# A fused attention and feed-forward kernel: fewer filler matmuls in slot 0, one turned product moved a slot later, one key copy moved behind a sum

## The chip, the cores and the metric

The kernel runs on one core of one Trainium2 chip. The metric is the device time of one execution in microseconds, the median of several runs. Besides the runs there is one profiled execution, whose trace is read here.

## The reference

Inputs are q, k, v of shape 8 x 8 x 576 x 64 (batch, heads, sequence, head width), a forget gate f of 8 x 8 x 576, and two weight matrices, 512 x 2048 and 2048 x 512. Cut to what matters:

```python
scores = scale * q @ k.T                          # per batch and head
cum = np.cumsum(np.log(np.clip(f, 1e-4, 1)), -1)
decay = cum[..., :, None] - cum[..., None, :]
attn = softmax(where(causal, -1e9, scores + decay))
x = (attn @ v) -> (8 * 576, 8 * 64)               # heads side by side
h = x @ w_in
out = (h - tanh(h)) @ w_out                       # 4608 x 512, float32
```

## The kernel before

**Slots.** A pair is two heads of one batch element; there are 32 pairs, four to a batch element (NPAIR = 4). The main loop at the end of the kernel goes over slots p = 0, 1, 2, ...; slot p emits the work of pair p. `att_items(p)` writes that work as a list of items by hand, going over the seven score tiles of a pair (ti = 0 to 6). Between the items the loop deals out pieces of the feed-forward part (the list `mlp`): how many a slot gets is in `TAKE`, and `first` says after how many counted items the dealing begins. Nothing is reordered afterwards: each engine runs its instructions in the order in which they are emitted, and waits on semaphores for its inputs and for buffers to come free. Slots 0 to 3 (batch element 0) have no feed-forward work yet, since it needs the finished attention of batch element 0; it begins in slot 4.

**One pair.** `trans` turns the queries or keys of a pair on TensorE (six transposing matmuls, L298) into a PSUM bank, and two copies, for the even and the odd positions, bring the bank into QT or KT (L309 on ScalarE, L311 on VectorE). The string `copies` names the engines: V is VectorE, A is ScalarE. With "VA" only the first copy is emitted at once and the second is put on the list `LATER`, which `rest` empties; with other strings both are emitted at once. `scores` multiplies (L352; in batch element 0 a second matmul, L355, adds the causal mask), and ScalarE takes the exponential into an e tile (L361; el is the small fourth tile). From batch element 1 on GpSimd masks e instead (L371). `values` multiplies e with v (L389) and then has VectorE divide by the row sums in three steps: L398 (rs), L399 (reciprocal), L400 (xn, the product of the pair).

**Turning the products.** The feed-forward part needs xn with the features on the partitions. In batch element 0 `turn` does this with five transposing matmuls (L417) into a bank and one copy into the ring XR, on VectorE when it is called with `vector=True` (L419), else on ScalarE (L421). In later batch elements a transposing DMA does it. The four pairs of batch element 0 fill XR chunks 0 to 3. Before the change pair 0 is turned in slot 2, pair 1 in slot 3 (both by VectorE), pair 2 and pair 3 in slot 4 (by ScalarE and VectorE).

**Feed-forward.** `mlp1(u, ft)` projects 512 tokens (block u) onto 128 hidden features with four matmuls, one for each XR chunk (L451, hps); ScalarE takes tanh (L456, th), and VectorE forms the gated sum gq = hps + th, with th = tanh(-h) (L462). The first two units, (0, 0) and (0, 1), are split in slot 4: part 0 does the matmuls of chunks 0 to 2, and part 1, at ti = 4 and 5, the one of chunk 3, tanh and sum. `mlp2_plain` and `mlp2` (L492, L517) multiply with the second weights. The PSUM banks m0 to m2 go round among turned tiles and projections through `m_bank`; scores go round two banks "sc" and one bank "tr".

**Unread matmuls.** `unread(n)` issues n matmuls of 128 x 128 on a constant tile into the bank "tr" (L566, idle <- warm); nobody reads the result. They stand at the start (47, 6, 38, 2) and in slot 0 (6, 4, 10 after the tiles ti = 2, 5, 6).

**Loads.** All loads of q, k, v and the weights are DMAs that GpSimd's queue issues in program order between its masks; SyncE issues the small rows, the transposing DMAs and the output.

Of the kernel before, what the change touches and what calls it, by code (L numbers as in the profile page):

```python
# [21 lines left out]
def kernel(  # L22
# [18 lines left out]
    NPAIR = H // 2  # L41
# [28 lines left out]
    def m_bank(name):  # L70
        while M_AT[0] % 3 in KEPT:
            M_AT[0] += 1
        M_AT[0] += 1
        return ps_m.tile([P, 512], FP32, tag=f"m{(M_AT[0] - 1) % 3}", name=name)

    def keep():
        while M_AT[0] % 3 in KEPT:
            M_AT[0] += 1
        KEPT.append(M_AT[0] % 3)
# [13 lines left out]
    qn, kn = ([t[0:S // NT6, :].rearrange("p (h n d) -> p h n d", h=H, n=NT6) for t in raw] for raw in (qraw, kraw))  # L93
# [3 lines left out]
    KT = [qkp.tile([D + 3, H, PITCH], FP16, tag=f"KT{i}", name=f"KT{i}") for i in range(2)]  # L97
# [100 lines left out]
    def load_aug(b):  # L198
        for to, of in aug_rows(b):
            nc.sync.dma_start(out=to, in_=of)  # L200

    def const_rows(i):
        h0 = 1 - i
        nc.sync.dma_start(out=QT[i][D:D + 2, h0:H, :], in_=minus16[0:2 * (H - h0), :])
        nc.sync.dma_start(out=KT[i][D + 2:D + 3, h0:H, 0:S], in_=ones16[0:H - h0, :])
# [81 lines left out]
    def trans(b, c, src, dst, early, copies, split=False):  # L287
        pn, g3 = S // NT6, NT6 // 2
        if early:
            t32 = m_bank("t32")  # L290
        elif KEPT and src is kn:
            t32 = ps_m.tile([P, UW], FP32, tag=f"m{KEPT[0]}", name="t32")
        else:
            t32 = ps_tr.tile([P, UW], FP32, tag="tr", name="t32")
        t16 = t32.bitcast(FP16)[:, 0:2 * S // 2].rearrange("p (a g n) -> p a g n", a=2, g=g3)
        for a in range(2):
            for g in range(g3):
                nc.tensor.transpose(out=t16[:, a, g, :],  # L298
                                    in_=src[b % 2][:, 2 * c + a, 2 * g:2 * g + 2, :],
                                    identity=id16[0:pn, 0:pn])  # L300
        parts = [(a, e) for a in range(2) for e in range(2)] if split else [(slice(0, 2), e) for e in range(2)]

        def copy(a, e, eng):
            if split:
                a = slice(a, a + 1)
            to = dst[b % 2][0:D, 2 * c:2 * c + 2, e:S:2].rearrange("d a (p g) -> d a p g", g=g3)[:, a]
            of = t16[e * D:(e + 1) * D, :, :, :].rearrange("d a g p -> d a p g")[:, a]
            if eng == "A":
                nc.scalar.activation(out=to, in_=of, func=AF.Copy)  # L309
            else:  # L310
                nc.vector.tensor_copy(out=to, in_=of)  # L311

        todo = [lambda a=a, e=e, eng=eng: copy(a, e, eng) for (a, e), eng in zip(parts, copies)]
        now = 1 if copies == "VA" else 2
        for fn in todo[:now]:
            fn()
        if copies == "VA":
            LATER.extend(todo[now:])
        return todo[now:]

# [117 lines left out]
    def widen(n):  # L438
        turn_of[:] = [n, 0]
# [123 lines left out]
    def unread(n):  # L563
        idle = ps_tr.tile([P, UW], FP32, tag="tr", name="idle")
        for i in range(n):
            nc.tensor.matmul(out=idle[:, i % 4 * P:i % 4 * P + P], lhsT=warm, rhs=warm, start=True, stop=True)  # L566

    pairs = [(b, c) for b in range(B) for c in range(NPAIR)]

    def start():  # L570
        unread(47)
        nc.scalar.activation(out=QT[0][NH:NX, 0, :], in_=cum[NH:NX, :], func=AF.Identity, bias=add_q[NH:NX, :], scale=mul_q[NH:NX, :])
        q_rest = trans(*pairs[0], qn, QT, True, "AAAA", True)
        for fn in q_rest:
            fn()
        unread(6)
        k_rest = trans(*pairs[0], kn, KT, True, "VVVV", True)
        unread(38)
        scores(*pairs[0], 0)
        for fn in k_rest:  # L580
            fn()
        scores(*pairs[0], 1)
        unread(2)
# [7 lines left out]
    def att_items(p):  # L591
        def put(fn, *args):
            items.append((lambda: fn(*args), True))

        items = []
        here = pairs[p] if p < len(pairs) else None
        before = pairs[p - 1] if 0 < p <= len(pairs) else None
        after = pairs[p + 1] if p + 1 < len(pairs) else None
        early = p < NPAIR
        for ti in range(len(TILES)):  # L600
            if here and (p > 0 or ti > 1):
                put(scores, *here, ti)
            if p == 1 and ti == 6:
                items.append((lambda: const_rows(1), False))
                items.append((lambda: load_aug(1), False))
            if p == 0 and ti in (2, 5, 6):
                put(unread, {2: 6, 5: 4, 6: 10}[ti])
            if p == 1 and ti == 3:
                put(last)
            for load in LOADS.get((p, ti), ()):  # L610
                items.append((load, False))
            at_q, at_k = (1, 2) if p == 0 else (None, 0) if early else (0, 2) if p == NPAIR else (0, 3)
            if ti == 5 and p < NPAIR - 1:
                put(trans, *pairs[p + 2], qn, QT, True, "VV")
            if p in (2 * NPAIR - 1, 2 * NPAIR, 2 * NPAIR + 1) and (ti % 2 or ti == 0):
                items.append((rest, False))
            if p in (2 * NPAIR - 1, 2 * NPAIR) and ti % 2 == 0:
                pair = pairs[2 * NPAIR + 2 * (p - 2 * NPAIR + 1) + ti // 4]
                put(trans, *pair, *((kn, KT) if ti % 4 else (qn, QT)), False, "VA")
            if ti == at_q and p < 2 * NPAIR - 1:  # L620
                put(trans, *after, qn, QT, early, "VV")
            if p == NPAIR:
                if ti in (4, 5):
                    put(mlp1, 0, ti - 4, 1)
            if ti == at_k and p < 2 * NPAIR - 1 and p != NPAIR:
                put(trans, *after, kn, KT, early, "AV" if p in (0, 2) else "VV")
            if p == NPAIR:
                if ti == 1:
                    put(turn, *pairs[p - 2])
                    put(values, *before)  # L630
                    put(mlp1, 0, 0, 0)
                elif ti == 2:
                    put(mlp1, 0, 1, 0)
                    put(turn, *before, True)
                    put(trans, *after, kn, KT, early, "VV")
            elif early and ti in (2, 4) and before:
                put(values, *before, (ti // 2 - 1,))
            elif not early and ti == 2 and before:
                put(values, *before, (0, 1), p == NPAIR + 2)
            if p < NPAIR:  # L640
                if ti == 1 and p > 1:
                    put(turn, *pairs[p - 2], True)
            elif p > NPAIR and ti == 3:
                items.append((release, False))
                put(turn, *before)
        return items
# [4 lines left out]
    TAKE = (0, 0, 0, 0, 2, 7, 6, 6, 6, 8, 8, 7, 7)  # L651
    at = 0
    start()
    bulk()
    for p in range(len(pairs) + 1):
        b, c = divmod(p, NPAIR)
        items = att_items(p)
        take = TAKE[p] if p < len(TAKE) else 8 - (p - len(TAKE)) % 2
        if p == 2 * NPAIR - 1:
            keep()  # L660
        if p == 2 * NPAIR + 1:
            KEPT.clear()
            widen(1)
        mine = mlp[at:at + take]
        at += take
        first = 14 if p == NPAIR else 0
        if p == len(pairs):
            for fn, *args in mine[0:2]:
                fn(*args)
            mine = mine[2:]  # L670
        given, n = 0, 0
        whole = sum(counts for _, counts in items)
        for emit, counts in items:
            emit()
            n += counts
            while n > first and given < len(mine) and given * (whole - first) < (n - first) * len(mine):
                fn, *args = mine[given]
                fn(*args)
                given += 1
# [31 lines left out]
```

## Time and profile before

| | |
|---|---|
| time, median of 3 runs | 339.54 us (339.47 to 339.68) |
| profiled execution, its own time | 339.82 us |
| its span, first to last instruction | 338.1 us |
| TensorE (PE) busy | 331.3 us, 98% |
| VectorE (DVE) busy | 261.6 us, 77% |
| ScalarE (ACT) busy | 232.9 us, 69% |
| GpSimd (POOL) busy | 162.3 us, 48% |

Busy times are of the span of the profiled execution; what lies around the span (1.7 us) is not in the trace. Slot 0 begins near 9.5 us, pair 1's scores at 14.31, pair 2's at 17.65, pair 3's at 21.78, pair 4's at 25.71 and pair 5's at 34.22. In the lines of the trace PE is the matmuls, PEld TensorE's weight loads. "out<-in" names the tiles; x10 behind an operation means ten of them merged into one line. The line numbers are those of the kernel before.

### The profile page before, as it was taken

The page shows a single profiled execution, that of the slowest core. Times are in us where ns is not written, and L with a number is a line of the kernel's source. Part 1 is how long each engine was busy: PE and PEld are TensorE (multiplying, and loading weights), DVE is VectorE, ACT ScalarE, POOL GpSimd, SP SyncE. Part 2 cuts the span into 40 slices and gives each one's busy share as a digit, 9 for nine tenths or more (in the row PEclk, how much of TensorE's full clock was granted, in tenths as well). Part 3 has the DMA queues.
Part 4 walks back from the last instruction along what each step waited for, and adds up shares of the span by engine and source line. Part 5 has one row for each costly group of instructions (what it writes and reads, how often), then busy time and mean ns, then how long its engine had stood idle before and what let it go on. Part 6 is the DMA issues. An engine that isn't in the chain of part 4 may idle for free.

```text
span 338.1 us, 8750 instructions
## 1 busy us (share of the span) xinstructions
PE 331.3 (98%) x3325; PEld 237.7 (70%) x3325; DVE 261.6 (77%) x510; ACT 232.9 (69%) x437; POOL 162.3 (48%) x321
## 2 busy tenths in 40 slices
PE   8998999999999999999999999999999999999996
PEld 8875558875587558855888888656875686486485
DVE  7899886659888887778867796688667866966865
ACT  6896777978977886778677867787558733632630
POOL 8977467775667574777377637632322210000000
PEclk9999999999999999999999999999999999999999
DMA  9999999999969997999899999990130222002003
GB/s 112 143 202 201 186 198 170 172 156 168 141 88 169 153 134 81 133 181 135 100 110 186 129 115 110 168 132 16 50 114 3 19 66 95 2 31 95 1 12 114
DMA packets 147468, 38.82 MB, mean 115 GB/s; under 512 B 128181, under 2 KB 146335, under 8 KB 147426
## 3 DMA queue, kind: packets, MB, share of 16 engines
q0 software_dynamic: 94528, 18.37, 74.3%
q1 hardware_dynamic: 52892, 19.89, 32.5%
q8 instruction: 26, 0.43, 0.6%
q14 instruction: 16, 0.13, 0.2%
q10 hardware_dynamic: 6, 0.01, 0.0%
HBM read 36.85 MB, written 9.44 MB: 137 GB/s over the span
## 4 chain that ended last, share of the span: by engine, by line
PE 95%; DVE 2%; ACT 2%; issue 0%; ACTq 0%
PE hps L451 36%; PE ops L517 29%; PE ps L352 12%; PE av L389 8%; PE ops L492 4%; PE idle L566 3%; PE t L298 2%; ACT e L361 1%; DVE KT L311 1%; PE ps L355 0%; ACT KT L309 0%; PE x L417 0%; DVE XR L419 0%; DVE xn L400 0%; DVE QT L311 0%
## 5 line engine op out<-in xcount | busy, mean ns | idle before, releaser
L451 PE MATMUL hps<-XR,win 128*128 128x512 f16 (+1 forms) x640 | 140.7, 357 | 0.4 <-DVE gq L462 0.3
L456 ACT ACTIVATE th<-hps 128x512 f32<-128x512 f32 x144 | 86.7, 602 | 55.3 <-PE hps L451 52.3
L361 ACT ACTIVATE e<-ps 128x512 f16<-128x512 f32 x192 | 110.1, 597 | 9.8 <-PE ps L352 7.6
L462 DVE TENSOR_TENSOR gq<-hps,th 128x512 f16<-128x512 f32 x144 | 98.2, 687 | 23.5 <-ACT th L456 21.8
L371 POOL TENSOR_SCALAR_AFFINE_SELECT e<-e 128x128 f16<-128x128 f16 x168 | 59.9, 359 | 73.5 <-ACT e L361 71.4
L451 PEld LDWEIGHTS <-win 128*128 128x128 f16 x640 | 57.8, 97 | 48.9 <-issue 1.0
L352 PE MATMUL ps<-QT,KT 67*128 67x64 f16 (+4 forms) x384 | 76.5, 276 | 1.1 <-ACT e L361 0.8
L517 PEld LDWEIGHTS <-gq 128*128 128x128 f16 x640 | 60.3, 97 | 11.1
L517 PE MATMUL ops<-wout,gq 128*128 128x256 f16 x512 | 63.2, 272 | 0.0
L352 PEld LDWEIGHTS <-KT 67*128 67x128 f16 x384 | 36.5, 98 | 22.0 <-DVE KT L311 0.5
L389 PEld LDWEIGHTS <-e 128*128 128x128 f16 x896 | 32.3, 97 | 3.6
L389 PE MATMUL av<-vn,e 128*128 128x65 f16 x896 | 33.6, 193 | 0.0
L517 PE MATMUL ops<-W,sq 128*128 128x256 f16 x256 | 31.2, 272 | 0.0
L131 POOL DMA_DIRECT2D vn<-in_v_dram x32 | 28.0, 877 | 6.4 <-DMA win<-in_moe_w_in_dram 2.7
L400 DVE TENSOR_TENSOR xn<-av,rs 128x640 f16<-128x640 f32 x32 | 26.4, 825 | 1.3 <-DMA out_dram<-ost 0.2
L517 PEld LDWEIGHTS <-sq 128*128 128x128 f16 x256 | 24.2, 98 | 3.4
L108 POOL DMA_DIRECT2D kn<-in_k_dram x25 | 21.2, 846 | 2.1 <-issue 1.8
L108 POOL DMA_DIRECT2D qn<-in_q_dram x25 | 21.2, 846 | 1.8 <-issue 1.4
L371 POOL TENSOR_SCALAR_AFFINE_SELECT el<-el 128x128 f16<-128x128 f16 x28 | 9.3, 332 | 26.1 <-ACT el L361 25.9
L398 DVE TENSOR_SCALAR rs<-av 128x10 f32<-128x10 f32 x32 | 5.2, 163 | 18.4 <-PE av L389 17.3
L484 DVE TENSOR_TENSOR gq<-gq 128x512 f16<-128x512 f16 x32 | 17.1, 534 | 0.0
L532 ACT ACTIVATE m<-ops 128x512 f32<-128x512 f32 x16 | 9.5, 596 | 10.9 <-PE ops L517 10.9
(83 smaller groups left out, 316.2 us busy)
## 6 DMA issues: line engine op xcount, KB each, us to landing
out_dram<-ost SPq DMA_DIRECT2D x34, 256.0 KB
vn<-in_v_dram POOLq DMA_DIRECT2D x24, 128.0 KB, 6.0
qn<-in_q_dram POOLq DMA_DIRECT2D x20, 128.0 KB, 4.6
kn<-in_k_dram POOLq DMA_DIRECT2D x20, 128.0 KB, 5.3
win<-in_moe_w_in_dram POOLq DMA_DIRECT2D x2, 1024.0 KB, 11.6
wout<-in_moe_w_out_dram POOLq DMA_DIRECT2D x2, 1024.0 KB, 16.2
XR<-xn SPq DMA_TRANSPOSE x56
qn<-in_q_dram POOLq DMA_DIRECT2D x6, 144.0 KB, 4.8
```

The source lines that it names most:

```text
L108: nc.gpsimd.dma_start(out=dst[b % 2][0:pn, n, :].rearrange("p (h d) -> p h d", h=H), in_=src[b, :, n * P:n * P + pn, :].rearrange("h p d - ...
L131: nc.gpsimd.dma_start(out=vn[b % 2][:, n, h0:h1, 0:D], in_=v[b, h0:h1, n * P:(n + 1) * P, :].rearrange("h p d -> p h d"))
L352: nc.tensor.matmul(out=ps[:, col:col + n], lhsT=kt[0:rows, h, j * P:(j + 1) * P], rhs=qt[0:rows, h, i0:i0 + n], start=True, stop=cut == 0)
L361: nc.scalar.activation(out=e[:, lo:hi], in_=ps[:, lo:hi], func=AF.Exp, bias=-SHIFT, scale=qscale)
L371: nc.gpsimd.affine_select(out=view, in_=view, compare_op=ALU.is_ge, fill=0.0, base=0, pattern=pat, channel_multiplier=-1)
L389: nc.tensor.matmul(out=av[:, a, ib, :], lhsT=E.pop((b, c, a, j, ib)), rhs=vn[b % 2][:, j, 2 * c + a, 0:D + 1], start=(j == 0), stop=(j == ib))
L400: nc.vector.tensor_tensor(out=xn.rearrange("p i (a d) -> p a i d", a=2), in0=av[:, :, :, 0:D], in1=rs.to_broadcast([P, 2, NJ, D]), op=ALU. ...
L451: nc.tensor.matmul(out=hps[:, o:o + n], lhsT=win[:, ci, ft * P:(ft + 1) * P], rhs=XR[:, ci, t:t + n], start=(ci == 0), stop=(ci == NCH - 1))
L456: nc.scalar.activation(out=th, in_=hps, func=AF.Tanh, scale=-1.0)
L462: nc.vector.tensor_tensor(out=GQ[(u, i)][:, half, kt, :], in0=hps, in1=th, op=ALU.add)
L484: nc.vector.tensor_tensor(out=LHS[name](u, i)[:, ks], in0=LHS[x](u, i)[:, ks], in1=LHS[y](u, i)[:, ks], op=op)
L517: nc.tensor.matmul(out=ps[:, m, :], lhsT=LHS[lhs](u, kt // 4)[:, kt % 4, m * P:(m + 1) * P], rhs=rhs[:, kt, :], start=(fresh and (apart or ...
```

## The change

There are three edits.

1. `unread(38)` ahead of the first scores becomes `unread(34)`, and the 10 unread matmuls after the last score tile of slot 0 become 2: twelve fewer.
2. Pair 1's product is turned in slot 4, at ti = 0 behind the scores and the turned queries of that place, instead of in slot 3 at ti = 1; its copy into XR is done by ScalarE instead of VectorE. As slot 4 thereby has one more counted item, `first` goes from 14 to 15.
3. The copies of pair 5's turned keys, in slot 4 at ti = 2, are marked "Vv": the first is emitted at once, the second goes on `LATER` and is emitted by `rest` behind `mlp1(0, 0, 1)` at ti = 4, so on VectorE it stands behind the first gated sum instead of ahead of it. It stays on VectorE.

```diff
@@ trans
-        now = 1 if copies == "VA" else 2
+        now = 1 if copies in ("VA", "Vv") else 2
         for fn in todo[:now]:
             fn()
-        if copies == "VA":
+        if now == 1:
             LATER.extend(todo[now:])
@@ start
         k_rest = trans(*pairs[0], kn, KT, True, "VVVV", True)
-        unread(38)
+        unread(34)
         scores(*pairs[0], 0)
@@ att_items
             if p == 0 and ti in (2, 5, 6):
-                put(unread, {2: 6, 5: 4, 6: 10}[ti])
+                put(unread, {2: 6, 5: 4, 6: 2}[ti])
...
             if p == NPAIR:
                 if ti in (4, 5):
                     put(mlp1, 0, ti - 4, 1)
+                    items.append((rest, False))
...
             if p == NPAIR:
-                if ti == 1:
+                if ti == 0:
+                    put(turn, *pairs[1])
+                elif ti == 1:
                     put(turn, *pairs[p - 2])
                     put(values, *before)
                     put(mlp1, 0, 0, 0)
                 elif ti == 2:
                     put(mlp1, 0, 1, 0)
                     put(turn, *before, True)
-                    put(trans, *after, kn, KT, early, "VV")
+                    put(trans, *after, kn, KT, early, "Vv")
...
             if p < NPAIR:
-                if ti == 1 and p > 1:
-                    put(turn, *pairs[p - 2], True)
+                if ti == 1 and p == 2:
+                    put(turn, *pairs[0], True)
@@ the loop over slots
-        first = 14 if p == NPAIR else 0
+        first = 15 if p == NPAIR else 0
```

## The prediction

> **What bounds the kernel now.** I read the page first (busy time, chain), then the stretches of time, then who TensorE waits for, then the timelines of TensorE and VectorE where those waits lie. The page:
> ```profile
> PE 331.3 (98%) x3325; PEld 237.7 (70%) x3325; DVE 261.6 (77%) x510; ACT 232.9 (69%) x437; POOL 162.3 (48%) x321
> PE 95%; DVE 2%; ACT 2%; issue 0%; ACTq 0%
> ```
> TensorE is the chain. Whatever it gains early it keeps, if nothing later is tied to the clock on the wall. The stretches (core, then PE, PEld, DVE, ACT, POOL busy, clock, DMA):
> ```profile
> 9.50:14.30 4.80, 4.50 (x65) 3.62 (x63) 3.92 (x7) 4.13 (x8) 4.80 (x8) 1.00 1.27 152
> 14.30:20.20 5.90, 5.54 (x104) 4.68 (x104) 5.51 (x9) 5.25 (x12) 5.78 (x11) 1.00 1.61 177
> 20.20:25.70 5.50, 5.11 (x93) 4.23 (x93) 5.25 (x10) 5.17 (x12) 3.34 (x5) 1.00 1.15 207
> 25.70:30.10 4.40, 3.69 (x52) 2.33 (x51) 4.17 (x9) 2.73 (x5) 2.38 (x3) 1.00 1.62 193
> 30.10:33.40 3.30, 2.94 (x26) 1.65 (x26) 2.75 (x5) 2.37 (x7) 3.29 (x8) 1.00 1.12 214
> 33.40:338.10 304.70, 301.17 (x2888) 212.84 (x2887) 232.51 (x451) 206.75 (x388) 134.36 (x274) 1.00 1.06 109
> ```
> From 33.4 us on TensorE is busy for 301.17 of 304.70 us. Slots 0 to 4, where the whole change lies, are different: TensorE idles 2.1 of 23.9 us, and VectorE is the fullest engine from 14.3 to 30.1. TensorE's own waits name the places:
> ```profile
> PE ps L352 <- ACT e L361: 0.8, 2, 0.4
> PE x L417 <- DVE xn L400: 0.7, 1, 0.7
> PE hps L451 <- DVE gq L462: 0.3, 1, 0.3
> ```
> VectorE's timeline (start, length, and in brackets the idle time before) shows it back to back from 16.97 on:
> ```profile
> 12.59 0.81 DVE L311 COPY KT<-t 64x576 f16<-64x576 f16 x1 [0.33 <-ACT KT L309]
> ...
> 16.97 0.17 DVE L398 TENSOR_SCALAR rs<-av 128x10 f32<-128x10 f32 x1 [0.28 <-PE av L389]
> ...
> 20.56 0.46 DVE L419 COPY XR<-x 128x576 f16<-128x576 f16 x1
> 21.10 0.17 DVE L398 TENSOR_SCALAR rs<-av 128x10 f32<-128x10 f32 x1
> ...
> 25.57 0.46 DVE L419 COPY XR<-x 128x576 f16<-128x576 f16 x1
> 25.95 0.16 DVE L398 TENSOR_SCALAR rs<-av 128x10 f32<-128x10 f32 x1
> ...
> 30.98 1.61 DVE L311 COPY KT<-t 64x576 f16<-64x576 f16 x2
> 32.61 1.31 DVE L462 TENSOR_TENSOR gq<-hps,th 128x512 f16<-128x512 f32 x2
> ```
> So slots 1 to 3 are paced by VectorE's queue, and TensorE's turns at 27.27 and 30.11 wait for its last product, xn. TensorE's timeline in slot 0 and at the gated sums:
> ```profile
> 7.36 2.29 PE L566 MATMUL idle<-warm 128*128 128x128 f16 x38
> 9.49 0.38 PE L352 MATMUL ps<-QT,KT 67*128 67x512 f16 x1
> ...
> 13.54 0.72 PE L566 MATMUL idle<-warm 128*128 128x128 f16 x10
> 14.31 0.38 PE L352 MATMUL ps<-QT,KT 67*128 67x512 f16 x1
> ...
> 33.36 1.02 PE L451 MATMUL hps<-XR,win 128*128 128x512 f16 x4 [0.35 <-DVE gq L462]
> ```
>
> **Four unread matmuls before the first scores.** 7.36 to 9.49 for 38 is 56 ns each; four are 0.22. The scores behind them need the first two of four key copies (L311, four in 1.98 from 8.16, so two by 9.14). They would start at 9.27, just clear. ScalarE's exponentials wait for these scores (start 9.96, 0.57 idle before), so ScalarE too is 0.22 earlier, and the key copy at 12.59, which waits for ScalarE.
>
> **Eight at the end of slot 0.** 8 x 56 ns = 0.45, and with the first 0.22 pair 1's scores go from 14.31 to 13.65. Their key copy ends at 13.40 - 0.22 = 13.18, in time. ScalarE's exponential at 14.78 had waited 0.45; now ScalarE is free at 14.33 - 0.22 = 14.11 and the scores end at 14.08, so it starts near 14.12: 0.66 gained. VectorE does not get all of it. It is full until 16.69 - 0.22 = 16.47, so the 16.97 step comes at 16.50 (0.47). At 21.10 there is a further gap of 0.08 behind the XR copy, and the step can also tuck under that copy's tail, as it does at 25.95 (0.38 behind the copy's start): 20.56 - 0.47 + 0.38 = 20.47. TensorE's product, which that step also needs, is ready by 21.07 - 0.66 = 20.41. VectorE has gained 0.63.
>
> **Pair 1's turn.** VectorE loses the XR copy at 25.57; what followed started 0.38 later, so 0.38 is gained: 0.63 + 0.38 = 1.01 on xn for pairs 2 and 3, and so on TensorE's turns (27.27 to 26.26, 30.11 to 29.10). The five turning matmuls (0.28 by the spacing at 27.27) now stand before TensorE's 0.69 wait and cost nothing there. ScalarE takes a copy of 0.65 (its L421 row) between two exponentials of slot 4. In order: exponential to about 26.05, pair 1's copy to 26.65, exponential to 27.2, pair 2's copy to 27.8. The projection's third matmul, the first to need the latter, is due at 28.90 - 1.01 = 27.89. Cover: 0.1 there, and another 0.1 before the turn at 29.10, so up to 0.2 of lateness is free; beyond that it costs one for one. If ScalarE had come into slot 4 with only 0.22, the loss would be about 0.25.
>
> **The second key copy behind the first gated sum.** In times of before: the tanh ends at 32.22, the sum would run 32.26 to 32.95 instead of 32.61 to 33.31, and TensorE's 0.35 at 33.36 goes. But the copy (0.80) then holds the second sum to 34.38 (was 33.92). The projection unit at 34.44 needs that bank; it would arrive at 34.09 and wait until 34.43. So the wait moves one unit on: 0.0. Ends: 0.35 gained if the second sum is no bound, 0.1 lost if the copy makes the pair 5 scores late (they are due at 33.9, the copy ends at 33.7). I take 0.0, since both ends of that step are in rows. The pacing constant 14 to 15 only makes up for the added step.
>
> **Sum.** 0.63 + 0.38 + 0.0 = 1.0. The profiled execution took 339.82 (span 338.1 and 1.7 around it), 0.28 above the median of 339.54; 338.8 for it, 338.5 for the median. Check: 12 x 56 ns = 0.67 less for TensorE and 0.33 less idle, out of 2.1.
>
> A measurement of this kernel can tell about 0.2% (0.68 us) from no change; the forecast is 0.3%.
>
> **Rivals.** *Half of it* (338.9): ScalarE is the late one in slot 4, or VectorE gets little from the eight matmuls. Gain 0.4 to 0.85. For it: covers of 0.1. Chance 0.17, of which 0.06 beyond 0.2%.
>
> *Held by a transfer* (339.4): the slots are early but data are not. For it: GpSimd's queue is full of DMAs that do not move with TensorE; it waits 2.66 at 26.21 for the first win, and the last v block (issued 29.36, 8.5 to landing) lands at 37.9, only 0.1 before pair 4's product comes to its fourth block at 38.0. Were that product waiting for it, 0.1 would be all. Against: these blocks hold heads 2 to 7, pair 4 needs heads 0 and 1 (issued 20.44 and 21.19, 9.2 to landing: 30.4). First win lands at 25.9 and is used at 28.47; the batch 2 keys land at 50.8 and are turned at 54.66. Chance 0.11.
>
> [...] The first 47 took 5.19, 110 ns each, against 56 ns from 6.6 on, so a low rate exists, lasted 5.1 us, and the clock column (1.00 throughout) does not show it. If as long a low stretch came back in slots 0 to 1, where TensorE is nearly always busy, half of it, 2.55, would be lost: 339.54 - 1.0 + 2.55 = 341.1. [...] Against: the largest gap in slot 0 stays at 0.4 (12.31 to 12.72), and the 0.69 wait at 27.27 was followed by turning matmuls at 58 ns. Chance 0.07, with 0.02 for other losses.
>
> [...]
>
> **Numbers.** Forecast (gain 0.85 to 1.35) 0.63; half 0.17; held 0.11; slower 0.09. Faster by over 0.2%: 0.63 + 0.06 = 0.69; within: 0.11 + 0.11 = 0.22; slower 0.09. The range 338.2 to 339.4 goes from the 0.35 of the gated sum on top of the forecast to the held case, and leaves out the slower ones and half of that case.
>
> **What would show it.** Right: 34 and 2 unread matmuls in their rows; pair 1's first scores near 13.65; VectorE's L398 steps near 16.5, 20.5 and 24.95; TensorE's turns near 26.3 and 29.1; the wait on gq smaller at the fourth unit, with a like one at the fifth; one more L421 row of 0.65; PE from there to the end as long as before (304.7 from 33.4). Wrong: matmuls at 110 ns after 9.5 (clock); a TensorE wait on ACT XR L421, or on a DMA of v; or a stretch after 34 us longer than before.

## The result and the profile after

The changed kernel takes 338.86 us (median of 14 runs, 338.76 to 339.19) against 339.53 us before: 0.67 us less, a ratio of 0.998 with a 95% interval of 0.9972 to 0.9988. The forecast was 338.5. The direction was right, the size was two thirds of what was forecast. An unchanged time lies outside the interval, and the forecast's own ratio, 0.997, just below it.

The two profiled executions differ by more than the medians: spans of 338.1 and 337.1 us, their own times 339.82 and 338.77, 1.05 us apart. The page of the changed kernel:
```profile
PE 330.0 (98%) x3313; PEld 235.6 (70%) x3313; DVE 260.8 (77%) x509; ACT 233.2 (69%) x438; POOL 163.2 (48%) x321
PE 90%; DVE 7%; ACT 2%; issue 1%; ACTq 0%
```
The chain now runs through VectorE for 7% where it was 2%. Followed back, it lies on VectorE almost throughout from 0.9 to 9.1 us, where it lay on the unread matmuls before, and again from 12.2 to 26.0, where before it did so only from 23.1 to 27.2: TensorE has less filler of its own, so VectorE's queue paces slots 1 to 3. From the fifth projection unit on nothing is new. For the prediction's last stretch the row of the changed kernel, with the window moved 1.00 us earlier, is (in the form of the prediction's stretches):
```profile
32.40:337.10 304.70, 300.81 (x2887) 212.47 (x2884) 232.62 (x452) 206.29 (x388) 136.36 (x276) 1.00 1.07 110
```
Its length is set by the choice of the window and shows nothing; TensorE is busy for 300.81 us in it, 301.17 before. That the gain was kept is seen from the fifth unit: from its start to the end of the span are 303.7 us in both (34.44 to 338.1, and 33.38 to 337.1). From TensorE's list of waits after the change (us in total, times, longest):
```profile
PE ps L352 <- DVE KT L311: 1.4, 2, 0.9
PE hps L451 <- DVE gq L462: 0.3, 1, 0.3
PE x L417 <- DVE xn L400: 0.2, 1, 0.2
```
The wait on xn fell from 0.7 to 0.2, the wait on the gated sum is as long as it was, and the first line is new. Its second piece, 0.43, stands at pair 4's scores (24.78), which waited 0.41 for an exponential before. Its longest piece is at the very start, in TensorE's timeline:
```profile
6.13 2.06 PE L566 MATMUL idle<-warm 128*128 128x128 f16 x34
9.12 0.39 PE L352 MATMUL ps<-QT,KT 67*128 67x512 f16 x1 [0.92 <-DVE KT L311]
...
31.82 1.02 PE L451 MATMUL hps<-XR,win 128*128 128x512 f16 x4
...
33.38 1.02 PE L451 MATMUL hps<-XR,win 128*128 128x512 f16 x4 [0.32 <-DVE gq L462]
```
The 34 unread matmuls are over at 8.2, and the first scores wait 0.92 us for the key copies: here the four that were left out had not been on the path at all. At the other end the fourth unit (33.36 before) starts without a wait at 31.82, and the fifth now waits 0.32. VectorE's timeline between them:
```profile
16.35 0.17 DVE L398 TENSOR_SCALAR rs<-av 128x10 f32<-128x10 f32 x1
...
20.28 0.17 DVE L398 TENSOR_SCALAR rs<-av 128x10 f32<-128x10 f32 x1
...
24.75 0.17 DVE L398 TENSOR_SCALAR rs<-av 128x10 f32<-128x10 f32 x1
...
31.08 0.69 DVE L462 TENSOR_TENSOR gq<-hps,th 128x512 f16<-128x512 f32 x1 [0.49 <-ACT th L456]
31.80 0.81 DVE L311 COPY KT<-t 64x576 f16<-64x576 f16 x1
32.64 1.29 DVE L462 TENSOR_TENSOR gq<-hps,th 128x512 f16<-128x512 f32 x2
```
Against before (16.97, 21.10, 25.95) the divisions are 0.62, 0.82 and 1.20 us earlier, and TensorE's turns (27.27 and 30.11 before) come at 26.09 and 28.94, 1.18 and 1.17 earlier. Of this 0.37 is already there at the first scores (9.49 to 9.12). At the fifth unit 1.06 is left (34.44 to 33.38). ScalarE takes its new copy between two exponentials, as foreseen:
```profile
25.75 0.65 ACT L421 ACTIVATE XR<-x 128x576 f16<-128x576 f16 x1
26.29 0.59 ACT L361 ACTIVATE e<-ps 128x512 f16<-128x512 f32 x1
26.77 0.66 ACT L421 ACTIVATE XR<-x 128x576 f16<-128x576 f16 x1
```
So two things had to be settled: whether the 0.37 at the start belongs to the change, and whether the third edit cost something.

### The profile page after: what moved, and what is told of

The parts are those of the page before. It is cut to its first block, busy times and chain, and to the rows that moved or that the text cites. A ratio compares the mean times of both kernels' runs of the same rounds, so it can differ in the third digit from the quotient of the medians.

```text
span 337.1 us, 8726 instructions
## 1 busy us (share of the span) xinstructions
PE 330.0 (98%) x3313; PEld 235.6 (70%) x3313; DVE 260.8 (77%) x509; ACT 233.2 (69%) x438; POOL 163.2 (48%) x321
## 4 chain that ended last, share of the span: by engine, by line
PE 90%; DVE 7%; ACT 2%; issue 1%; ACTq 0%
PE hps L451 36%; PE ops L517 29%; PE ps L352 11%; PE av L389 8%; PE ops L492 4%; DVE KT L311 2%; DVE QT L311 1%; PE t L298 1%; ACT e L361 1%; DVE xn L400 1%; DVE gq L462 0%; DVE TQ L187 0%; ACT th L456 0%; PE x L417 0%; DVE clo L190 0%
## 5 line engine op out<-in xcount | busy, mean ns | idle before, releaser
L371 POOL TENSOR_SCALAR_AFFINE_SELECT e<-e 128x128 f16<-128x128 f16 x168 | 60.7, 364 | 71.5 <-ACT e L361 68.7
```

The costliest lines, as they stand in the source:

```text
L371: nc.gpsimd.affine_select(out=view, in_=view, compare_op=ALU.is_ge, fill=0.0, base=0, pattern=pat, channel_multiplier=-1)
```

## The experiments

The median of before was 339.52 or 339.53 in each comparison. "Beside" a value is always that of the same set of runs.

**The kernel before, profiled a second time.** No edit.

> The kernel before, unchanged, for a second profile. Theory A (clock): TensorE's rate doubles at a different moment in each execution (7.1 us in the first profile of before, 4.0 us in that of after). If it doubles before about 6.4 us, the 38 unread matmuls end before the key copies do, and the first scores start near 9.15 behind a wait on the key copies, with a span near 337.8; if it doubles near 7 they start near 9.49 with a span near 338.1. Theory B (no such thing): the rate doubles near 7.1 again, first scores at 9.49, span 338.1.

Measured: 339.60, span 337.9. TensorE's timeline:
```profile
7.13 2.29 PE L566 MATMUL idle<-warm 128*128 128x128 f16 x38
9.25 0.38 PE L352 MATMUL ps<-QT,KT 67*128 67x512 f16 x1
```
The same program reaches its first scores 0.24 us earlier than in the first profile, because the matmuls ahead of it came 56 ns apart sooner, from 6.4 us on instead of 7.0. Theory A, between its two cases: the unread matmuls still end last, but earlier. The moment at which TensorE's matmuls come to stand 56 ns apart instead of 107 is read from the timeline of each execution:

| execution | rate doubles at | first scores at | span | its own time |
|---|---|---|---|---|
| before, first profile (38 unread) | 7.0 | 9.49 | 338.1 | 339.82 |
| before, second profile (38) | 6.4 | 9.25 | 337.9 | 339.60 |
| eight fewer, below (38) | 4.2 | 9.12 | 337.3 | 339.14 |
| four fewer, below (34) | 4.1 | 9.12 | 337.8 | 339.47 |
| changed kernel (34) | 4.1 | 9.12 | 337.1 | 338.77 |
| changed kernel, second profile (34) | 5.5 | 9.12 | 337.1 | 338.85 |
| changed without the third edit, second profile (34) | 7.1 | 9.33 | 337.2 | 338.94 |

In the rows with a rise by 5.5 us the first scores stand at 9.12 with 34 and with 38 unread matmuls; with a rise near 7 they stand at 9.33 with 34 and at 9.49 with 38. With 38 and an early rise, in the profile of the kernel with eight fewer at the end of slot 0:
```profile
6.15 2.29 PE L566 MATMUL idle<-warm 128*128 128x128 f16 x38
9.12 0.39 PE L352 MATMUL ps<-QT,KT 67*128 67x512 f16 x1 [0.68 <-DVE KT L311]
```
In 11 of the 14 profiles taken here the first scores start at 9.11 to 9.13, three of these with 38 unread matmuls. The first profile of before had a late rise, at 7.0.

**Only the four unread matmuls ahead of the first scores.**
```diff
-        unread(38)
+        unread(34)
```


> Only the four unread matmuls ahead of the first scores are left out (38 to 34). Theory A: in most executions the first scores wait for VectorE's key copies and not for the unread matmuls, so the median moves by 0.0 to 0.1 us (339.45 to 339.55). Theory B: they are on the path in every execution, 0.22 us faster (339.3).

Measured: 339.54 beside 339.52, ratio 0.9998 (0.9989 to 1.0007). In its profile the first scores wait for the key copies:
```profile
9.12 0.39 PE L352 MATMUL ps<-QT,KT 67*128 67x512 f16 x1 [0.86 <-DVE KT L311]
```
The four matmuls are worth nothing in the median. The ratios on record are not exactly the quotients of the medians; the two differ by up to 0.0005, so differences below about 0.15 us need more than one set of runs.

**Only the eight unread matmuls at the end of slot 0.**
```diff
-                put(unread, {2: 6, 5: 4, 6: 10}[ti])
+                put(unread, {2: 6, 5: 4, 6: 2}[ti])
```


> Only the eight unread matmuls at the end of slot 0 are left out (10 to 2). Theory A: ScalarE starts pair 1's exponentials 0.45 us earlier and VectorE passes 0.3 to 0.45 of it on: 339.1 to 339.25. Theory B (VectorE's queue swallows it): under 0.15 us faster, 339.4 or more.

Measured: 339.13 beside 339.52, 0.39 less, ratio 0.9984 (0.9975 to 0.9993). Theory A: VectorE passes on most of the 0.45.

**Only the turn of pair 1.** The second edit with `first` at 15; unread matmuls and key copies as before.

> Only pair 1's turn is moved to slot 4 and its copy given to ScalarE. Theory A: VectorE's next product is 0.38 us earlier and ScalarE's extra 0.65 us copy is covered: 0.3 to 0.4 us faster, 339.15 to 339.25. Theory B (ScalarE becomes the late one in slot 4, since here it has not gained from slot 0): TensorE waits on the copy of pair 2's product, under 0.15 us faster.

Measured: 339.15 beside 339.52, 0.37 less, ratio 0.9988 (0.9979 to 0.9996). Theory A; TensorE does not wait on ScalarE's copies: its waits from 24 to 35 us are 0.43 for a key copy, 0.16 for xn and 0.35 for a gated sum.

**Only the third edit.** "Vv" and the `rest` behind the first gated sum, in the kernel before.

> Only pair 5's second key copy is put behind the first gated sum, in the kernel before. Theory A (the wait only moves one unit on, and the copy does not tuck under the sum's tail): the wait on gq leaves the fourth projection unit and returns at the fifth, which starts 0.1 us later than before; median 0.05 to 0.15 us slower (339.6 to 339.7). Theory B (the sum was the bound): 0.3 us faster (339.2).

Measured: 339.61 beside 339.52, 0.09 more, ratio 1.0002 (0.9993 to 1.001). The interval includes an unchanged time, so the median alone does not show it; the profile does, in that the fourth unit starts at 32.64 and the fifth at 34.20, where in the kernel with four fewer (first scores equally at 9.1) they start at 32.99 and 34.07. The wait moves a unit on: the fourth comes 0.35 earlier, the fifth 0.13 later.

**The changed kernel without the third edit.**
```diff
-                    put(trans, *after, kn, KT, early, "Vv")
+                    put(trans, *after, kn, KT, early, "VV")
```


> The changed kernel without the move of pair 5's second key copy (VV again). Theory A: the other two parts add up, 0.39 + 0.37 = 0.76 less than before, about 0.1 us faster than the changed kernel: 338.75, span near 336.95, and the fifth unit (hps) starts 0.1 us earlier than in the changed kernel. Theory B (the copy's place was worth something once VectorE is early): 0.2 to 0.3 us slower than the changed kernel, 339.1.

Measured: 338.69, ratio to before 0.9973 (0.9963 to 0.9982); the second time, beside the changed kernel:

> The changed kernel without the move of pair 5's second key copy, again. Theory A (the move costs 0.11 us at the fifth projection unit): 338.7, 0.1 to 0.2 us faster than the changed kernel in the same call. Theory B (the first difference of 0.17 us was noise): equal to it.

> The changed kernel again, beside the next two on the same chip: 338.8 to 338.9, first scores near 9.12 behind the key copies if the rate doubles before 6.4 us.

Measured: 338.72 against 338.87 for the changed kernel, ratios to before 0.9976 (0.9966 to 0.9986) and 0.9982 (0.9973 to 0.9991). The intervals overlap, but the difference came out twice (0.17 against 338.86, which is of another set of runs, and 0.15 within one set), and the sum of the two separate parts foresaw its direction. The first profile without the edit shows the wait back at the fourth unit and none at the fifth:
```profile
32.19 1.02 PE L451 MATMUL hps<-XR,win 128*128 128x512 f16 x4 [0.35 <-DVE gq L462]
...
33.27 1.03 PE L451 MATMUL hps<-XR,win 128*128 128x512 f16 x4
```
The fifth unit starts 0.11 earlier than in the changed kernel (33.38). This version is the fastest of all that were run.

**The copy on ScalarE behind the second tanh.** An attempt to keep both sums close together:
```diff
-                    put(trans, *after, kn, KT, early, "Vv")
+                    put(trans, *after, kn, KT, early, "VA")
...
-                if ti in (4, 5):
-                    put(mlp1, 0, ti - 4, 1)
-                    items.append((rest, False))
+                if ti == 4:
+                    put(mlp1, 0, 0, 1)
+                elif ti == 5:
+                    put(lambda: (mlp1(0, 1, 1), rest()))
```


> The changed kernel with pair 5's second key copy on ScalarE, behind the second tanh, so that VectorE's gated sums follow one another. Theory A (VectorE's copy between the sums is what holds the fifth unit): the second sum ends near 32.7 instead of 33.33, the fifth unit starts near 33.05 instead of 33.38; 0.25 to 0.35 us faster than the changed kernel, 338.55. Theory B (ScalarE then delays the third tanh and the pair 5 scores by as much): no faster than the changed kernel.

Measured: 339.26, 0.40 more than the changed kernel. The fifth unit does start earlier, at 33.13. VectorE then waits for the tanh behind the copy, though its third sum still starts before that of the changed kernel (34.05):
```profile
33.50 0.69 DVE L462 TENSOR_TENSOR gq<-hps,th 128x512 f16<-128x512 f32 x1 [0.77 <-ACT th L456]
```
TensorE keeps its lead of 0.25 until 40.2 (40.49 in the changed kernel) and loses it there:
```profile
42.02 0.87 PE L352 MATMUL ps<-QT,KT 67*128 67x320 f16 x3 [0.15 <-ACT e L361]
43.08 1.02 PE L451 MATMUL hps<-XR,win 128*128 128x512 f16 x4 [0.19 <-DVE gq L462]
```
The unit that the changed kernel starts at 42.69 starts at 43.08. The gain of 0.25 is lost and 0.39 more. That is theory B's outcome; how the copy on ScalarE leads to the waits near 42 us was not followed, so its mechanism is not shown.

**Pair 1's copy on VectorE, still in slot 4.**
```diff
-                    put(turn, *pairs[1])
+                    put(turn, *pairs[1], True)
```


> The changed kernel, but the copy of pair 1's turned product, still in slot 4, is done by VectorE again. Theory A (VectorE's queue paces slots 1 to 4, so the engine is what counts, not the slot): the copy lands ahead of pair 3's division, which and TensorE's turn of pair 3 come 0.35 to 0.45 us later; 0.3 to 0.4 us slower than the changed kernel, 339.2 to 339.25. Theory B (the later slot is enough, VectorE idles 0.55 us before pair 3's copy there): within 0.1 us of the changed kernel.

Measured: 339.34 beside 338.87, 0.47 more. The price is a little above theory A's 0.3 to 0.4: the copy stands ahead of pair 3's division on VectorE, and it is also late for the projection that needs pair 1's chunk:
```profile
28.11 0.59 PE L451 MATMUL hps<-XR,win 128*128 128x512 f16 x2 [0.45 <-DVE XR L419]
```
The later slot alone earns nothing; the copy has to leave VectorE. Whether a copy on ScalarE in slot 3 would do as well was not run.

**Eight unread matmuls ahead of the first scores, twice.**
```diff
-        unread(34)
+        unread(8)
```


> The changed kernel with 8 instead of 34 unread matmuls ahead of the first scores: TensorE stands idle for 2 to 2.5 us there. Theory A (the key copies pace that place and a rate once risen outlasts such a gap): same as the changed kernel within 0.1 us in most executions, 338.8 to 338.95. Theory B (the fillers hold the clock up): matmuls at 107 ns again after 9 us, 0.5 to 2.5 us slower than the changed kernel.

> Eight unread matmuls ahead of the first scores, again. Theory A (the key copies pace that place; TensorE's 0.49 us wait near 73 us for a transposing DMA in the first profile of it was chance): as the changed kernel within 0.1 us. Theory B (fewer fillers cost something): again 0.2 us slower or more in the median, with the DMA wait or with matmuls at 107 ns after 9 us.

Measured: 339.07 (338.75 to 339.81), 0.2 above the changed kernel and so outside what theory A allowed, and, beside 338.87, 338.92 (338.76 to 339.75), inside it. TensorE stands still for 2.27 us, and the matmuls behind it come at the higher rate all the same (six turning matmuls in 0.42, as at 7.11 in the first profile of before; the six at 6.12 there, ahead of the rise, took 0.69):
```profile
9.12 0.39 PE L352 MATMUL ps<-QT,KT 67*128 67x512 f16 x1 [2.27 <-DVE KT L311]
...
9.80 0.42 PE L298 MATMUL t<-id,qn 96*128 96x96 f16 x6
```
So the low rate did not come back, with far fewer fillers than the change leaves (8 against 34). The best runs equal those of the changed kernel; 8 of 22 took over 339.2, against 1 of 25 of the changed kernel. One long one was profiled (339.25, span 337.5), and its excess is a wait near 73 us, far from the edit, which holds TensorE up by 0.49:
```profile
73.37 0.38 PE L451 MATMUL hps<-XR,win 128*128 128x512 f16 x1 [0.32 <-DMA XR<-xn]
```
In five of the eight the span is no longer than that of the changed kernel (337.0 to 337.1): the excess lies around the span, 2.2 to 2.8 us in place of 1.7, where the trace shows nothing. In the other three the span is longer (337.5 to 337.7). No run of another kernel with its span on record has more than 1.84 around it. The median span is 337.1 in both sets, as in the changed kernel, so between first and last instruction theory A holds; why long runs are more frequent with eight unread matmuls stays open.

## Why the prediction was right or wrong

**Four unread matmuls: 0.22 forecast, 0.00 measured.** This is the step that failed. The prediction priced them on the profiled execution of before, where the unread matmuls ended just after the key copies, and took that for the rule. It also noted that this execution was 0.28 above the median, and subtracted the 0.28 at the end without asking where it lay. It lay right there: TensorE's rate had doubled late. The prediction put the 56 ns spacing at 6.6; its row of six unread matmuls at 6.60 takes 0.67, as against 0.50 for six behind the rise (6.54 in the second profile), and the rise came at 7.0. That in most executions the key copies were already the last is inferred from the spans: 337.8 in the profile of four fewer, where they were, and 337.8 in the median of before in each of the three sets that have spans, against 338.1 in its first profile. There nothing was left to gain. The moment of the rise differs between executions, 4.1 to 7.1 us in the table above, and the prediction took that of one execution for all.

**Eight unread matmuls: 0.41 forecast (the part of 0.45 that VectorE passes on), 0.39 measured alone.** The steps are visible in the profile: pair 1's scores at 13.50, that is 14.31 less the 0.37 of the start and 0.44; VectorE's divisions at 16.35 and 20.28, 0.25 and 0.45 beyond the start. (The prediction calls VectorE the fullest engine from 14.3 on; in its first stretch, to 20.2, GpSimd with 5.78 us and TensorE with 5.54 were fuller than VectorE with 5.51. No term rests on it.)

**Pair 1's turn: 0.38 forecast, 0.37 measured alone.** The third division stands at 24.75, 0.38 beyond what the second had gained, and ScalarE's cover was enough.

**The key copy behind the sum: 0.0 forecast, about 0.1 lost.** The mechanism was the foreseen one, the wait moves from the fourth unit to the fifth. The size was off by about 0.1. The prediction's sum ends at 32.95, and a copy of 0.80 and a second sum of 0.69 behind it would end at 34.44 if one followed the other; it has 34.38, so it counted on 0.06 of overlap, such as the query copies have behind other sums (36.74 before, where the sum ends at 36.82). In the run there were two gaps of 0.03 instead: the copy started at 31.80 behind a sum that ended at 31.77, and the second sum at 32.64 behind a copy that ended at 32.61. The lower end given in the prediction, 0.1 lost, is what came, though through the second sum and not through pair 5's scores.

**Sum.** 0.00 + 0.39 + 0.37 - 0.09 = 0.67, the measured difference. That it agrees to the hundredth is luck: the first three together, which are the changed kernel without the third edit, gave 0.83 and 0.80, not 0.76. Of the two profiled executions the 1.05 is 0.37 of the start and 0.68 of the change. Nearly all of the 0.37 is the moment of the rise (7.0 against 4.1 us); the key copies too began 0.07 later in the first profile of before (8.16, against 8.09 or 8.10 in all others), which the late unread matmuls covered.

**The rivals.** *Half of it* gave the right number, 338.9, for a wrong reason: neither was ScalarE late nor did VectorE swallow the eight. *Held by a transfer* did not come: pair 4's product began at 36.67 without a wait. The low stretch, the rival of 341.1, did not come back. That leaving out fillers could bring it back was the author's supposition, and the kernel with eight at the start speaks against it well beyond what this change does: behind its gap of 2.27 us six turning matmuls took 0.42, and none of its 22 spans is over 337.7.

## What to carry to other kernels

When the profiled execution is off the median by as much as the effects in question, find where it is off before pricing anything on it; the step that was last only in that execution was worth nothing in the median here. Removing fillers paid only where they were the last to be ready (eight at the end of slot 0: 0.39; four ahead of the first scores: 0.00), and the place to look is the engine that the next wait names: here VectorE's queue was back to back through slots 1 to 3, and moving one 0.46 us copy off it earned 0.37. A wait that is removed by swapping two instructions of one queue can come back at whoever needs the one that went second, as it did here (0.35 at the fourth unit before, 0.32 at the fifth after).

## What the runs showed of the hardware

The spacing of the unread matmuls fell from 107 to 56 ns early in each execution of the table above, and the moment differed: from 4.1 to 7.1 us, 2.9 to 6.0 us after the first matmul, though the program is the same up to the 34 or 38 unread matmuls. For one and the same program it was 6.4 and 7.0 (before) and 4.1 and 5.5 (the changed kernel). What sets the moment is not shown. The clock column of the stretches shows 1.00 throughout in the first profiles of before and of the changed kernel, also from 0 to 4 us, where the matmuls stand 107 ns apart; only their spacing tells. A gap in TensorE's work of 2.27 us, and one of 2.33 us in the second profile, did not bring the low rate back (eight unread matmuls ahead of the first scores).
